# Gated mix of linear attention and SwiGLU: the last output tile in two column groups of 448 and 64 instead of three, its first group evicted by two engines

## The chip, the cores and the metric

The kernel runs on one core of a Trainium2 chip. A core has five engines that run side by side and meet at semaphores: TensorE (PE in the profile: matmuls; PEld: the weight loads that go ahead of them), VectorE (DVE), ScalarE (ACT), GpSimd (POOL) and SyncE (SP), which here only issues DMAs. ScalarE can issue DMAs as well; ACTq and SPq are the two queues from which they are issued here. Matmuls write to PSUM[...] from which VectorE or ScalarE must copy ("evict") a result to SBUF[...].

The metric is the device time of one execution in microseconds (us); lower is better.

## The reference

All inputs and the output are bf16. The input x has 2048 rows (tokens) of 512 columns.

```python
x = A_x
g = _sigmoid((x * gate_w).sum(-1, keepdims=True))
a = _A_ref(x, A_wqkv, A_wo)      # linear attention, 32 heads of 16
b = _B_ref(x, B_w1, B_w3, B_w2)  # (silu(x @ w1) * (x @ w3)) @ w2, F = 1376
return g * a + (1 - g) * b

# _A_ref: q, k, v = x @ wqkv, split into heads
phi = lambda t: jnp.where(t > 0, t + 1, jnp.exp(t)) + 1e-6
pq, pk = phi(q), phi(k)
kv = jnp.einsum("bhsd,bhse->bhde", pk, v)
z = jnp.einsum("bhsd->bhd", pk)
num = jnp.einsum("bhqd,bhde->bhqe", pq, kv)
den = jnp.einsum("bhqd,bhd->bhq", pq, z)[..., None] + 1e-6
o = num / den                    # back to (S, D), then o @ wo
```

## The kernel before

The 2048 rows are 16 tiles of 128 (NT), in four blocks of 512 (NTB blocks, TPB = 4 tiles each). A first stage computes k for all tiles, phi(k), and the sum of x^T phi(k) over the rows; from it and the weights wv and wo it folds attention into one 512x512 matrix W_sb. Then each block runs the feed-forward part (emit_ffn: gate and up matmuls at L312 and L320, tanh on ScalarE, two VectorE operations that leave hT) and, tile by tile, the output (emit_out). Between these stands the preparation of the next block (emit_q, emit_rem, emit_den, emit_norm). After the last block's feed-forward there is nothing left to prepare, so the program ends with four calls of emit_out, for tiles 12 to 15, one behind the other.

TensorE's instructions are issued in the order in which the program writes them (a manual schedule for PE); the other engines follow by semaphores that a tile framework places, from which instruction reads or writes which buffer. An engine takes its instructions in its own fixed order: one that waits holds up those behind it.

emit_out computes a tile's 128x512 output as 15 matmuls that add up in one PSUM tile o_ps: four with the attention features (pqT by W_sb, L353), one with the remainder of F (hTr by w2r_sb, L357), ten with hT by w2_sb (L362). The factor omg, one value per row, is applied in the eviction. For tiles 0 to 14 this is one column group of 512, evicted by ScalarE (L367, row o_out) and stored by SP (L378, 128 KB). For the last tile (t = 15) the columns are cut into three groups, 0 to 256, 256 to 448 and 448 to 512, each with its own 15 matmuls, its own PSUM tile, its eviction and its store:

```python
parts = [(0, h, True), (h, q7, True), (q7, D, True)]      # L344: h = 256, q7 = 448
o_ps = psX.tile([P, b - a], FP32, tag=f"XP{2 + (tt + i) % 2}", name="o_ps")   # L351
eng = nc.scalar if i == 1 else nc.sync                    # L377
```

The groups' PSUM tiles alternate between the buffers XP3, XP2 and XP3. The first two groups are evicted by ScalarE (L367), the third by VectorE (L371, a tensor_scalar with omg). The first and third are stored from SP's queue, the second from ScalarE's (L378). The SBUF tile is o_last. The program ends (L509) when SP has seen every store landed and the engines have met at closing semaphores.

Of the kernel before, what the change touches and what calls it, by code (L numbers as in the profile page):

```python
# [8 lines left out]
ACT = mybir.ActivationFunctionType  # L9
ALU = mybir.AluOpType  # L10
# [3 lines left out]
BF16 = mybir.dt.bfloat16  # L14
# [3 lines left out]
def kernel(  # L18
# [12 lines left out]
    nc = tc.nc  # L31
    P = nc.NUM_PARTITIONS

    Bb, S, D = A_x.shape
# [4 lines left out]
    NT = S // P  # L39
# [10 lines left out]
    out2d = out.flatten_outer_dims()  # L50

    consts = ctx.enter_context(tc.tile_pool(name="consts", bufs=1))
# [26 lines left out]
    TF = 2  # L79
    x_first = x2d[0 : TF * P, :].rearrange("(p j) d -> p j d", j=TF)  # L80
    out_first = out2d[0 : TF * P, :].rearrange("(p j) d -> j p d", j=TF)
# [6 lines left out]
        out=xT[:, :, TF * P : TB], in_=x2d[TF * P : TB, :], transpose=True  # L88
    )
    for tb in range(1, NTB):  # L90
        dq.dma_start(
            out=xT[:, :, tb * TB : (tb + 1) * TB], in_=x2d[tb * TB : (tb + 1) * TB, :],
# [7 lines left out]
    with nc.allow_non_contiguous_dma(reason="one gate weight per partition and chunk"):  # L100
        dq.dma_start(
            out=wr_sb[:, :, 2 * FR : NR], in_=gate_w.rearrange("(kc d o) -> d kc o", d=P, o=1)
        )
    dq.dma_start(out=wv_sb[:], in_=wqkv_r[:, :, 2 * D : 3 * D])
    for fsl in (slice(0, FM // 2), slice(FM // 2, FM)):
# [13 lines left out]
        out=bm, in_=bm, pattern=[[-Dh, HPC], [0, Dh]], compare_op=ALU.is_ge, fill=0.0,  # L119
# [3 lines left out]
        out=bm, in_=bm, pattern=[[Dh, HPC], [0, Dh]], compare_op=ALU.is_ge, fill=0.0,  # L123
# [6 lines left out]
    omg = consts.tile([P, NT], FP32, name="omg")  # L130
# [171 lines left out]
    def emit_ffn(tb, fc, between=None):  # L302
# [30 lines left out]
            out=st[tb, "hT"][:, fc, :], in0=up_ps[:], in1=gs[:], op=ALU.mult  # L333
        )

    def emit_out(tb, tt):
        t = tb * TPB + tt
        tsl = slice(tt * P, (tt + 1) * P)

        if t < NT - 1:  # L340
            parts = [(0, D, True)]
        else:
            h, q7 = D // 2, 7 * D // 8
            parts = [(0, h, True), (h, q7, True), (q7, D, True)]  # L344
        if t < NT - 1:
            o_out = work.tile([P, D], BF16, tag="o_out", name="o_out")
        else:
            o_out = consts.tile([P, D], BF16, name="o_last")
        lo = 0
        for i, (a, b, store) in enumerate(parts):  # L350
            o_ps = psX.tile([P, b - a], FP32, tag=f"XP{2 + (tt + i) % 2}", name="o_ps")  # L351
            for c in range(KC):
                nc.tensor.matmul(  # L353
                    o_ps[:], lhsT=st[tb, "pqT"][:, c, tsl], rhs=W_sb[:, c, a:b],
                    start=(c == 0), stop=False,
                )
            nc.tensor.matmul(  # L357
                o_ps[:], lhsT=st[tb, "hTr"][:, tsl], rhs=w2r_sb[:, a:b],
                start=False, stop=False,
            )  # L360
            for fc in range(FC):
                nc.tensor.matmul(  # L362
                    o_ps[:], lhsT=st[tb, "hT"][:, fc, tsl], rhs=w2_sb[:, fc, a:b],
                    start=False, stop=(fc == FC - 1),
                )
            if i < 2:
                nc.scalar.activation(  # L367
                    out=o_out[:, a:b], in_=o_ps[:], func=ACT.Copy, scale=omg[:, t : t + 1]
                )
            else:  # L370
                nc.vector.tensor_scalar(  # L371
                    out=o_out[:, a:b], in0=o_ps[:], scalar1=omg[:, t : t + 1], scalar2=None,
                    op0=ALU.mult,
                )
            if store:
                rows = out_first[t] if t < TF else out2d[t * P : (t + 1) * P, :]
                eng = nc.scalar if i == 1 else nc.sync  # L377
                eng.dma_start(out=rows[:, lo:b], in_=o_out[:, lo:b])  # L378
                lo = b


    k0 = [psM.tile([P, D], FP32, tag="mm", name=f"k0_{t}") for t in range(TPB)]
# [21 lines left out]
    with tc.manual_schedule(engines={ENG.DVE}):  # L404
# [18 lines left out]
        for dc in range(KC):  # L423
# [9 lines left out]
            out=z_sb[:].rearrange("p (b f) -> p b f", f=Q),  # L433
            in_=z_col[:, :, None].to_broadcast([P, NB, Q]),
        )
        kvT_ps = psX.tile([P, KC, P], FP32, tag="XP0", name="kvT_ps")
        for c in range(KC):
# [7 lines left out]
            out=kvT_sb[:], in0=kvT_ps[:],  # L445
# [22 lines left out]
    for tb in range(NTB):  # L468
        for fc in range(FC if tb == 0 else 0, FC):
            emit_ffn(tb, fc)  # L470
        nx = tb + 1
        for tt in range(TPB):
            if nx < NTB:
                emit_q(nx, tt, psX, "XP0")
                if tt % 2 == 0:
                    emit_rem(nx, tt // 2, psX, "XP1")
                    if tt == 2:
                        emit_omg(nx)
            emit_out(tb, tt)
            if nx < NTB:  # L480
                emit_den(nx, tt)
        if nx < NTB:
            emit_norm(nx)
# [30 lines left out]
```

## Time and profile before

| what | value |
|---|---|
| median of 5 runs | 179.13 us (178.62 to 179.45) |
| profiled execution, its own time | 179.45 us |
| its span, first to last instruction | 177.7 us |
| TensorE clock granted | 0.998 |
| PE busy | 174.3 us, 98% of the span, 883 matmuls |
| DVE, ACT, POOL busy | 118.7, 65.5, 63.7 us |
| eviction of a 128x512 o_out (ACT) | 0.688 us |
| last tile's evictions | 0.473 (256, ACT), 0.421 (192, ACT), 0.284 (64, DVE) |
| store of 128 KB from issue to landing | 1.9 us, 15 of them |

Busy time is what an engine's instructions took; the span is what the profiler saw from the first to the last instruction, and the execution's own time is 1.7 us longer. A row of the profile names the line, the engine, the operation and what it writes and reads (out<-in). Durations of matmuls in rows are those of one matmul through the pipeline; in the chain of waits each step is only what it adds before the next can start, so a 512-column matmul is 379 ns in its row and about 216 ns in the chain. A row marked SPq or ACTq is the issue of a DMA by that engine's queue, not the transfer.

### The profile page before, as it was taken

The numbers are of one execution on the slowest core, as the hardware profiler recorded it, in microseconds if no ns is written. First come the engines' busy times: TensorE is split into PE (matmuls) and PEld (weight loads), VectorE is DVE, ScalarE is ACT, GpSimd is POOL, SyncE is SP. The second block draws the span as 40 slices with busy tenths as digits, with TensorE's granted clock in tenths as the row PEclk, the third lists the DMA queues.
The fourth block names the chain that finished last, engine by engine and source line by source line (L and its number), as shares of the span: only waits on it lengthen the run. The fifth ranks groups of instructions, "written<-read, shape, count | busy, mean of one in ns | idle before, by whom it ended". The sixth has DMA issues, their size and how long they took to land.

```text
span 177.7 us, 2473 instructions
## 1 busy us (share of the span) xinstructions
PE 174.3 (98%) x883; PEld 84.2 (47%) x883; DVE 118.7 (67%) x204; ACT 65.5 (37%) x123; POOL 63.7 (36%) x80
## 2 busy tenths in 40 slices
PE   8999999999999999999999999999999999999994
PEld 4444444474444545444454544444545444444463
DVE  0398667899999837498786375978764669786000
ACT  3542423476532333342333333342443333331222
POOL 6087765689154323262003232620032328100000
PEclk9999999999999999999999999999999999999999
DMA  5999999911005011123000111230001012200002
GB/s 171 221 308 226 295 325 360 348 58 29 10 0 115 3 44 33 44 59 89 0 0 10 38 37 37 59 90 6 0 7 50 24 51 74 63 0 0 30 30 63
DMA packets 30380, 15.14 MB, mean 85 GB/s; under 512 B 20928, under 2 KB 30240, under 8 KB 30368
## 3 DMA queue, kind: packets, MB, share of 16 engines
q1 hardware_dynamic: 29952, 14.67, 30.1%
q10 hardware_dynamic: 416, 0.31, 0.5%
q8 instruction: 7, 0.11, 0.3%
q14 instruction: 5, 0.04, 0.1%
HBM read 8.42 MB, written 2.10 MB: 59 GB/s over the span
## 4 chain that ended last, share of the span: by engine, by line
PE 98%; DVE 0%; issue 0%
PE o_ps L362 19%; PE up_ps L320 19%; PE gate_ps L312 19%; PE o_ps L353 8%; PE q_ps L217 8%; PE XP L204 8%; PE k_ps L184 6%; PE r_ps L241 3%; PE k L184 2%; PE o_ps L357 2%; PE warm L161 2%; PE kvT_ps L440 1%; PE W_ps L458 0%; PE xTp L174 0%; DVE o_last L371 0%
## 5 line engine op out<-in xcount | busy, mean ns | idle before, releaser
L320 PE MATMUL up_ps<-xT,w_sb 128*128 128x512 bf16 x160 | 41.1, 379 | 0.0
L312 PE MATMUL gate_ps<-xT,w_sb 128*128 128x512 bf16 x160 | 41.1, 379 | 0.0
L225 POOL TENSOR_TENSOR qz<-pq,z_sb 128x512 f32<-128x512 bf16 x16 | 18.5, 1161 | 58.0 <-DVE pq L145 58.0
L325 ACT ACTIVATE th<-gate_ps 128x512 bf16<-128x512 f32 x40 | 23.9, 597 | 39.1 <-PE gate_ps L312 38.7
L362 PE MATMUL o_ps<-w_sb,hT 128*128 128x512 bf16 (+3 forms) x180 | 37.5, 355 | 0.0
L327 DVE SCALAR_TENSOR_TENSOR gs<-th,gate_ps 128x512 bf16<-128x512 bf16 x40 | 27.3, 682 | 5.4 <-ACT th L325 5.1
L332 DVE TENSOR_TENSOR hT<-up_ps,gs 128x512 bf16<-128x512 f32 x40 | 27.7, 691 | 3.8
L142 DVE TENSOR_SCALAR phi_m<-phi_e 128x512 bf16<-128x512 bf16 x32 | 13.6, 426 | 21.7 <-ACT phi_e L140 21.6
L362 PEld LDWEIGHTS <-hT 128*128 128x128 bf16 x180 | 16.9, 98 | 17.8
L320 PEld LDWEIGHTS <-w_sb 128*128 128x128 bf16 x160 | 15.7, 98 | 18.9
L312 PEld LDWEIGHTS <-w_sb 128*128 128x128 bf16 x160 | 15.6, 98 | 18.6
L292 POOL TENSOR_TENSOR pqn<-pq,rden 128x512 bf16<-128x512 bf16 x16 | 16.5, 1055 | 15.1 <-DVE rden L285 13.1
L367 ACT ACTIVATE o_out<-o_ps,omg 128x512 bf16<-128x512 f32 x15 | 10.3, 688 | 28.9 <-PE o_ps L362 28.9
L194 POOL TENSOR_TENSOR pks<-pks,pk_sb 128x512 f32<-128x512 f32 x15 | 17.4, 1161 | 7.4 <-DVE pk_sb L145 6.7
L353 PE MATMUL o_ps<-W_sb,pqT 128*128 128x512 bf16 (+3 forms) x72 | 16.8, 355 | 0.0
L217 PE MATMUL q_ps<-wq_sb,xT 128*128 128x512 bf16 x64 | 16.4, 379 | 0.0
L204 PE MATMUL XP<-pk_sb,x_sb 128*128 128x512 bf16 x64 | 16.3, 379 | 0.0
L228 DVE TENSOR_REDUCE den<-qz 128x32 f32<-128x512 f32 x16 | 10.9, 684 | 7.9 <-POOL qz L225 7.8
L140 ACT ACTIVATE phi_e<-k_ps 128x512 bf16<-128x512 f32 x12 | 7.2, 597 | 14.4 <-PE k_ps L184 14.4
L140 ACT ACTIVATE phi_e<-q_ps 128x512 bf16<-128x512 f32 x16 | 9.6, 597 | 7.8 <-PE q_ps L217 7.7
L184 PE MATMUL k_ps<-wk_sb,xT 128*128 128x512 bf16 x48 | 12.3, 379 | 0.0
L145 DVE SCALAR_TENSOR_TENSOR pq<-q_ps,phi_m 128x512 bf16<-128x512 f32 x16 | 11.1, 691 | 0.5
(60 smaller groups left out, 120.8 us busy)
## 6 DMA issues: line engine op xcount, KB each, us to landing
w_sb<-in_B_w_dram SPq DMA_DIRECT2D x4, 640.0 KB, 8.7
out_dram<-o_out SPq DMA_DIRECT2D x15, 128.0 KB, 1.9
w_sb<-in_B_w_dram SPq DMA_DIRECT2D x1, 1280.0 KB, 11.7
x_sb<-in_A_x_dram SPq DMA_DIRECT2D x2, 512.0 KB, 4.3
x_sb<-in_A_x_dram SPq DMA_DIRECT2D x1, 768.0 KB, 5.1
wq_sb<-in_A_wqkv_dram SPq DMA_DIRECT2D x1, 512.0 KB, 4.9
wv_sb<-in_A_wqkv_dram SPq DMA_DIRECT2D x1, 512.0 KB, 6.0
wo_sb<-in_A_wo_dram SPq DMA_DIRECT2D x1, 512.0 KB, 11.1
```

The costliest lines, as they stand in the source:

```text
L184: nc.tensor.matmul(k_ps[:], lhsT=xT[:, kc, t * P : (t + 1) * P], rhs=wk_sb[:, kc, :], start=(kc == 0), stop=(kc == KC - 1),)
L194: nc.gpsimd.tensor_add(pks[:], pks[:], pk_sb[:, t, :])
L204: nc.tensor.matmul(XP_ps[dc][:], lhsT=x_sb[:, t, dc * P : (dc + 1) * P], rhs=pk_sb[:, t, :], start=(t == 0), stop=(t == NT - 1),)
L217: nc.tensor.matmul(q_ps[:], lhsT=xT[:, kc, ts_tok], rhs=wq_sb[:, kc, :], start=(kc == 0), stop=(kc == KC - 1),)
L225: nc.gpsimd.tensor_tensor(out=qz[:], in0=st[tb, "pq"][:, tt, :], in1=z_sb[:], op=ALU.mult)
L312: nc.tensor.matmul(gate_ps[:], lhsT=w1_sb[:, kc, fsl], rhs=xT[:, kc, tok_sl], start=(kc == 0), stop=(kc == KC - 1),)
L320: nc.tensor.matmul(up_ps[:], lhsT=w3_sb[:, kc, fsl], rhs=xT[:, kc, tok_sl], start=(kc == 0), stop=(kc == KC - 1),)
L325: nc.scalar.activation(out=th[:], in_=gate_ps[:], func=ACT.Tanh, scale=0.5)
L327: nc.vector.scalar_tensor_tensor(out=gs[:], in0=th[:], scalar=1.0, in1=gate_ps[:], op0=ALU.add, op1=ALU.mult)
L332: nc.vector.tensor_tensor(out=st[tb, "hT"][:, fc, :], in0=up_ps[:], in1=gs[:], op=ALU.mult)
L353: nc.tensor.matmul(o_ps[:], lhsT=st[tb, "pqT"][:, c, tsl], rhs=W_sb[:, c, a:b], start=(c == 0), stop=False,)
L362: nc.tensor.matmul(o_ps[:], lhsT=st[tb, "hT"][:, fc, tsl], rhs=w2_sb[:, fc, a:b], start=False, stop=(fc == FC - 1),)
```

## The change

Only emit_out is changed, and of what it emits only the last tile. The columns are cut into two groups, 0 to 448 and 448 to 512, with 15 matmuls each (30 where there were 45). The first group's PSUM tile (XP3) is evicted in two pieces: columns 0 to 256 by ScalarE, then stored from ScalarE's queue, and columns 256 to 448 by VectorE, then stored from SP's queue. The second group, of 64 columns (now in XP2), is evicted by VectorE and stored by SP, as its counterpart before. For tiles 0 to 14 the same instructions are emitted as before.

```diff
-        if t < NT - 1:
-            parts = [(0, D, True)]
+        last = t == NT - 1
+        h, q7 = D // 2, 7 * D // 8
+        groups = [(0, q7), (q7, D)] if last else [(0, D)]
+        pieces = (
+            {0: [(0, h, nc.scalar, nc.scalar), (h, q7, nc.vector, nc.sync)],
+             q7: [(q7, D, nc.vector, nc.sync)]}
+            if last
+            else {0: [(0, D, nc.scalar, nc.sync)]}
+        )
+        if last:
+            o_out = consts.tile([P, D], BF16, name="o_last")
         else:
-            h, q7 = D // 2, 7 * D // 8
-            parts = [(0, h, True), (h, q7, True), (q7, D, True)]
...
-        for i, (a, b, store) in enumerate(parts):
+        for i, (a, b) in enumerate(groups):
             o_ps = psX.tile([P, b - a], FP32, tag=f"XP{2 + (tt + i) % 2}", name="o_ps")
...
-            if i < 2:
-                nc.scalar.activation(
-                    out=o_out[:, a:b], in_=o_ps[:], func=ACT.Copy, scale=omg[:, t : t + 1]
-                )
-            else:
-                nc.vector.tensor_scalar(
-                    out=o_out[:, a:b], in0=o_ps[:], scalar1=omg[:, t : t + 1], scalar2=None,
-                    op0=ALU.mult,
-                )
-            if store:
-                rows = out_first[t] if t < TF else out2d[t * P : (t + 1) * P, :]
-                eng = nc.scalar if i == 1 else nc.sync
-                eng.dma_start(out=rows[:, lo:b], in_=o_out[:, lo:b])
-                lo = b
+            for lo, hi, evac, queue in pieces[a]:
+                if evac is nc.scalar:
+                    nc.scalar.activation(
+                        out=o_out[:, lo:hi], in_=o_ps[:, lo - a : hi - a], func=ACT.Copy,
+                        scale=omg[:, t : t + 1],
+                    )
+                else:
+                    nc.vector.tensor_scalar(
+                        out=o_out[:, lo:hi], in0=o_ps[:, lo - a : hi - a],
+                        scalar1=omg[:, t : t + 1], scalar2=None, op0=ALU.mult,
+                    )
+                queue.dma_start(out=out2d_rows(t)[:, lo:hi], in_=o_out[:, lo:hi])
```

out2d_rows(t) gives a tile's rows of the output, as the two branches did before.

More of the change, by code (lines that the diff above doesn't have):

```diff
@@ L334, in emit_ffn, with out2d_rows @@
         )
+    def out2d_rows(t):
+        return out_first[t] if t < TF else out2d[t * P : (t + 1) * P, :]
     def emit_out(tb, tt):
@@ L338, in emit_out @@
         tsl = slice(tt * P, (tt + 1) * P)
-        if t < NT - 1:
-            parts = [(0, D, True)]
-        else:
-            h, q7 = D // 2, 7 * D // 8
-            parts = [(0, h, True), (h, q7, True), (q7, D, True)]
-        if t < NT - 1:
+        last = t == NT - 1
[9 more added lines that the diff above has]
+            o_out = consts.tile([P, D], BF16, name="o_last")
+        else:
             o_out = work.tile([P, D], BF16, tag="o_out", name="o_out")
-        else:
-            o_out = consts.tile([P, D], BF16, name="o_last")
-        lo = 0
-        for i, (a, b, store) in enumerate(parts):
+        for i, (a, b) in enumerate(groups):
             o_ps = psX.tile([P, b - a], FP32, tag=f"XP{2 + (tt + i) % 2}", name="o_ps")
@@ L365, in emit_out @@
                 )
-            if i < 2:
-                nc.scalar.activation(
-                    out=o_out[:, a:b], in_=o_ps[:], func=ACT.Copy, scale=omg[:, t : t + 1]
-                )
-            else:
-                nc.vector.tensor_scalar(
-                    out=o_out[:, a:b], in0=o_ps[:], scalar1=omg[:, t : t + 1], scalar2=None,
-                    op0=ALU.mult,
-                )
-            if store:
-                rows = out_first[t] if t < TF else out2d[t * P : (t + 1) * P, :]
-                eng = nc.scalar if i == 1 else nc.sync
-                eng.dma_start(out=rows[:, lo:b], in_=o_out[:, lo:b])
-                lo = b
+            for lo, hi, evac, queue in pieces[a]:
[10 more added lines that the diff above has]
+                queue.dma_start(out=out2d_rows(t)[:, lo:hi], in_=o_out[:, lo:hi])
     k0 = [psM.tile([P, D], FP32, tag="mm", name=f"k0_{t}") for t in range(TPB)]
```

## The prediction, made before the result was known

> **What bounds the kernel now.** I read the clock view first (0.998, so no throttling has to be allowed for), then the page's chain of waits: TensorE carries 98% of it, so only two things can change the time, the length of the TensorE stream and what comes behind its last matmul. The change touches the last output tile alone, so I read the last seven microseconds. The chain in order of time, whose columns are start in us, length in us and what ran:
>
> ```profile
> 170.96 0.86 PE o_ps L362 x4
> 171.82 0.44 PE o_ps L353 x4
> 172.26 0.11 PE o_ps L357
> 172.37 1.09 PE o_ps L362 x10
> 173.46 0.33 PE o_ps L353 x4
> 173.79 0.08 PE o_ps L357
> 173.88 0.82 PE o_ps L362 x10
> 174.70 0.12 PE o_ps L353 x4
> 174.82 0.03 PE o_ps L357
> 174.84 0.31 PE o_ps L362 x10
> 175.15 0.03 issue
> 175.18 0.28 DVE o_last L371
> ```
>
> The reader is to see three groups of 15 matmuls without a gap: 256 columns in 1.64 us (0.44+0.11+1.09), 192 in 1.23 us, 64 in 0.46 us. The last ends at 175.15. Behind it stand one short eviction by VectorE and a store. The evictions and store issues, from the timeline by engine (start, length):
>
> ```profile
> 173.50 0.47 ACT L367 ACTIVATE o_last<-o_ps,omg 128x256 bf16<-128x256 f32 x1 [0.95 <-PE o_ps L362]
> 174.74 0.42 ACT L367 ACTIVATE o_last<-o_ps,omg 128x192 bf16<-128x192 f32 x1 [0.76 <-PE o_ps L362]
> ...
> 174.00 0.33 SPq L378 DMA_DIRECT2D out_dram<-o_last  x1
> ...
> 175.19 0.36 ACTq L378 DMA_DIRECT2D out_dram<-o_last  x1
> 175.49 0.33 SPq L378 DMA_DIRECT2D out_dram<-o_last  x1
> ```
>
> Each group's eviction and store lie under the next group's matmuls; after 175.15 only the 64-column eviction (0.28) and its store are bare. The table of DMA issues (KB, us from issue to landing) and SP's own waits close the picture:
>
> ```profile
> out_dram<-o_last SPq DMA_DIRECT2D x1, 64.0 KB, 2.1
> out_dram<-o_last ACTq DMA_DIRECT2D x1, 48.0 KB, 1.6
> out_dram<-o_last SPq DMA_DIRECT2D x1, 16.0 KB, 1.4
> ...
> SPq L509 <- DMA out_dram<-o_last: 0.6, 1, 0.6
> ```
>
> The 48 KB store lands at 175.19+1.6 = 176.8, the 16 KB one at 175.49+1.4 = 176.9, and the program's end (L509) waits for both. From 176.9 to the span's end at 177.7 there is a fixed 0.8 us of closing semaphores that the change leaves alone. So the end is set by when SP issues its last store.
>
> **What the Trainium skill says.** "PSUM — Partial Sum Buffer", section "PSUM bank collisions raise a hardware error": two engines may not access one bank on the same partitions at once, reads against reads included, and software has to guard a bank with semaphores. The trace of before has no two engines reading one o_ps tile, so it can neither confirm nor deny this; but it decides whether the two pieces of the 448 group can be evicted side by side. "VectorE: DVE Perf Modes", section "Why PSUM operands drop a tier": an fp32 PSUM operand keeps VectorE at its basic rate, and its "Specifications" give 0.96 GHz, so 128 more columns cost an estimated 0.133 us. The trace agrees roughly: the row gsr (L251, 128x192) takes 0.345 us and pq (L145, 128x512) 0.691, or 0.139 us for 128 columns. "DMA: Bandwidth & Descriptors", section "Issuing engines are not separate DMA queues": a second issuing queue saves only issue time. Here that is 0.33 us a store.
>
> **The change part by part.**
>
> TensorE. The 256 and 192 groups become one of 448. From the rows, a 512-column matmul advances the chain by 0.216 us (0.86/4), a 256-column one by 0.109 (1.64/15); on the line between them 448 columns cost 0.189, and 15 of them 2.84 us, against 1.64+1.23 = 2.87. Gain 0.03 us. The 15 weight loads that go were hidden (the row PEld is always beside PE). The 448 group ends at 174.67, the 64 group at 175.12. The 64 group now takes the PSUM buffer XP2 instead of XP3; its earlier owner is the tile before, evicted from 171.86 to 172.55, long before 174.67, so this wait costs nothing, and PE doesn't stop.
>
> ScalarE. It starts the 256-column piece 0.04 us behind the group as before (173.46 to 173.50): at 174.71, ends at 174.71+0.47 = 175.18. Before, the same piece was done at 173.97, under matmuls. It loses the 192 piece (0.42).
>
> VectorE. In the changed program's instruction order the 192-column eviction does not wait for PE but for ScalarE, and the semaphore's value is the one that the 256 piece sets. So the pieces run one behind the other, as the PSUM page asks. A wait of VectorE on ScalarE costs 0.03 us (phi_e 21.24+0.60, phi_m at 21.87), so it starts at 175.21. Its length isn't in the trace: the 64-column row of the same operation takes 0.284, and 128 columns more cost 0.139 or 0.133: 0.42. Bounds: 0.345, the row of that width at L251, and 0.45. I take 0.42, so it ends at 175.63. Queued behind it on VectorE is the 64-column eviction, whose matmuls are ready at 175.12 and which ran at 175.18 before. Independent VectorE instructions overlap by 0.08 us in the timeline (gsr 38.57+0.34, next at 38.83), so it ends at 175.84, or at 175.94 if it follows with a 0.03 gap. SP waits for it.
>
> SP. The 256 store leaves SP's queue for ScalarE's: it issues at 175.21 instead of 174.00. With the longest landing that the table shows for 64 KB, 2.1, it lands at 177.3. The 192 store moves from ScalarE's queue to SP's: SP starts 0.03 us behind an eviction (175.46, 175.49), hence 175.66, and is busy with it until 175.99. Only then can the 64 store be issued. Between two SP issues, the second of which also waits for its own DMA semaphore, the timeline shows 0.09 us (a transpose from 131.43 for 2.40 ends at 133.83, the next store starts at 133.92). So 175.99+0.09 = 176.08. The 64 eviction, ready at 175.84 to 175.94, hides under this.
>
> Sum. The last store is issued at 176.08 instead of 175.49: +0.59 us. With 1.4 us to landing it lands at 177.5, behind the 256 store (177.3), so that one is covered by 0.2 us. The chain of additions to compare: -0.03 (TensorE), then the 256 eviction 0.47, wait 0.03, 192 eviction 0.42, SP issue 0.33 and gap 0.09, in place of the 64 group and its eviction. The span goes from 177.74 to 178.33 and the profiled execution from 179.45 to 180.04; the median of the five runs, 179.13, is 0.32 lower than that execution, and the same addition gives 179.72 us, +0.33%.
>
> Unknowns: the 192 eviction (-0.08 to +0.03); SP's second issue, which took 0.53 instead of 0.33 where a store followed close behind transposes (row 133.92 in the timeline), 0 to +0.2; landing of a 16 KB store right behind a 48 KB one on its own queue, not in the trace. Before, the 16 KB store had 48 KB of another queue ahead of it, 0.30 us earlier, so I take 1.4 again, with -0.3 to +0.3 around it.
>
> **The rivals.** What a measurement of this kernel can tell from no change is about 0.3%, 0.54 us; the forecast stands just outside.
>
> A, the same mechanism with dearer stores: the second issue takes 0.53 and the landing is 0.2 longer, as three stores now end together with 128 KB in flight instead of 64. 179.13+0.59+0.2+0.2 = 180.1. For it: landings of the 128 KB o_out stores reach 3.3 us. Against: the DMA share at the end is low, 0.31 from 176 to 177 us.
>
> B, not slower: the end is carried by completion. The 192 store goes through SP's queue 0.42 us ahead of the 64 one and leaves the DMA rings running, so the last store lands sooner after its issue. If 1.4 becomes 0.8, the move of 0.59 is paid back: 179.13+0.59-0.60 = 179.1. It decides from a landing under 0.81 us. Against it: no store of o_out or o_last landed under 1.4.
>
> C, the wait doesn't bind: the two pieces are evicted side by side. Then VectorE's 192 piece runs from 174.71 to 175.13, the SP issues stand at 175.16 and 175.58 (+0.09), and the 256 store, 175.21+2.1 = 177.3, is the later by 0.4 in the worst case: 179.2 to 179.5. Against it: the wait is in the program.
>
> **How the numbers follow.** The serial chain at its own price, +0.4 to +0.75: 0.74, of which 0.52 comes out above 0.54 us as measured and 0.22 within it, since the medians themselves move by about 0.2 (runs from 178.62 to 179.45). A: 0.12, all slower. B: 0.07, of which 0.02 faster by over 0.3%, 0.05 within. C: 0.07, within. Slower 0.64, same 0.34, faster 0.02. Forecast 179.72. The range leaves out B's lower part and A's upper one: 179.3 to 180.15.
>
> **What would show each step right or wrong.** The 448 matmuls advancing by 0.189 us and the stream ending 0.03 earlier; the 192 eviction starting 0.03 behind the 256 one's end and not beside it; its length near 0.42; the SP stores 0.42 apart, the second at about 176.1; the 64 eviction finished before SP is free; landing of the last store near 1.4, and the tail of 0.8 unchanged. The prediction is wrong if VectorE starts at 174.7, if the stores land in under 1 us, or if the 256 store on ScalarE's queue lands last.

## The result, and the profile after

| | before | with the change |
|---|---|---|
| median | 178.97 us (80 runs, 178.49 to 179.85) | 179.66 us (43 runs, 179.11 to 181.3) |
| ratio to before | | 1.0041, 95% interval 1.0031 to 1.0050 |
| profiled execution, span | 179.45, 177.7 us | 179.79, 178.1 us |

The change makes the kernel slower by 0.4%, some 0.7 us. A ratio of 1 lies outside the interval. The five runs that the prediction started from had a median of 179.13; 80 runs give 178.97.

The chain of waits of the changed kernel, in order of time (start in us, length, what):

```profile
172.47 1.91 PE o_ps L368 x10
174.38 0.03 issue
174.40 0.48 ACT o_last L374
174.88 0.03 issue
174.91 0.42 DVE o_last L379
175.33 0.19 DVEq L513
```

Before, the chain ran through TensorE to the last matmul and left it for one eviction of 0.28 us. Now it leaves TensorE one column group earlier, at 174.38, goes through ScalarE's 256 columns, and then, behind them, through VectorE's 192. The last group's matmuls are no longer on it. (DVEq L513 is the end of VectorE's program, which comes when the 64-column eviction is done.) The timeline by engine:

```profile
174.20 0.28 PE L359 MATMUL o_ps<-W_sb,pqT 128*128 128x64 bf16 x4
...
174.40 0.47 ACT L374 ACTIVATE o_last<-o_ps,omg 128x256 bf16<-128x256 f32 x1 [2.15 <-PE o_ps L368]
174.91 0.42 DVE L379 TENSOR_SCALAR o_last<-o_ps,omg 128x192 bf16<-128x192 f32 x1 [11.81 <-ACT o_last L374]
...
174.91 0.36 ACTq L383 DMA_DIRECT2D out_dram<-o_last  x1
...
175.35 0.33 SPq L383 DMA_DIRECT2D out_dram<-o_last  x1
...
175.78 0.38 SPq L383 DMA_DIRECT2D out_dram<-o_last  x1
```

The bracket on the DVE row is the line to look for: VectorE had been idle for 11.81 us and was released by ScalarE's o_last, not by PE. SP's two stores stand 0.43 us apart.

The span depends on the whole program, its start too: in this execution the last tile began 0.30 us earlier than in the profile of before. To compare ends I therefore count from an event just ahead of the change, SP's issue of the store of tile 14, which is line one of before and line two of after:

```profile
172.58 0.33 SPq L378 DMA_DIRECT2D out_dram<-o_out  x1
```

```profile
172.28 0.33 SPq L383 DMA_DIRECT2D out_dram<-o_out  x1
```

Counted from there (the common clock of what follows), with the trace's nanoseconds, the last store is issued at 2.91 us before and 3.50 after (+0.59), it lands 1.44 and 1.48 us later (+0.04; landings on this clock are counted to the end of SP's closing wait for them, 0.02 us behind the landing itself), and the span ends at 5.16 and 5.81 (+0.65). So 0.59 of the 0.65 is already there when the last store is issued. TensorE itself is 0.035 us earlier (its last matmul starts at 2.331 instead of 2.366).

One profile is one execution, but the span of every execution is on record, to 0.1 us: 109 of before and 44 of the change. The mean span grows from 177.29 to 177.88, by 0.59 us (95% interval 0.45 to 0.73, by resampling the executions). The mean time grows by 0.72, so 0.13 of it lies outside the span. That part of an execution was 1.76 us on average before and never over 1.9; with the change it is 1.89 on average, and over 1.9 in 16 of the 44 executions. No trace covers it and its cause stays open. It is seen in e2, e3, e4, e5 and e7 below, whose last tile has 30 matmuls as in the change, and not in e1 and e6, which have 45 as before.

### The profile page after: what moved, and what is told of

Read it like the earlier page. It is cut to its first block, busy times and chain, and to the rows that moved or that the text cites. A ratio compares the mean times of both kernels' runs of the same rounds, so it can differ in the third digit from the quotient of the medians.

```text
span 178.1 us, 2442 instructions
## 1 busy us (share of the span) xinstructions
PE 173.8 (98%) x868; PEld 82.3 (46%) x868; DVE 120.3 (68%) x205; ACT 65.0 (36%) x122; POOL 63.6 (36%) x80
## 4 chain that ended last, share of the span: by engine, by line
PE 94%; DMA 3%; SPq 0%; ACT 0%; DVE 0%; issue 0%; DVEq 0%
PE gate_ps L312 19%; PE up_ps L320 19%; PE o_ps L368 19%; PE XP L204 8%; PE q_ps L217 8%; PE o_ps L359 8%; PE k_ps L184 6%; PE r_ps L241 3%; DMA xT<-in_A_x_dram 3%; PE o_ps L363 2%; PE k L184 1%; PE kvT_ps L444 1%; PE W_ps L462 0%; ACT o_last L374 0%; DVE o_last L379 0%; SPq L84 0%
## 5 line engine op out<-in xcount | busy, mean ns | idle before, releaser
L368 PE MATMUL o_ps<-w_sb,hT 128*128 128x512 bf16 (+2 forms) x170 | 37.3, 367 | 0.0
L142 DVE TENSOR_SCALAR phi_m<-phi_e 128x512 bf16<-128x512 bf16 x32 | 15.2, 475 | 20.1 <-ACT phi_e L140 20.1
L368 PEld LDWEIGHTS <-hT 128*128 128x128 bf16 x170 | 16.0, 98 | 18.6
L359 PE MATMUL o_ps<-W_sb,pqT 128*128 128x512 bf16 (+2 forms) x68 | 16.6, 366 | 0.0
```

The source lines that it names most:

```text
L359: nc.tensor.matmul(o_ps[:], lhsT=st[tb, "pqT"][:, c, tsl], rhs=W_sb[:, c, a:b], start=(c == 0), stop=False,)
L368: nc.tensor.matmul(o_ps[:], lhsT=st[tb, "hT"][:, fc, tsl], rhs=w2_sb[:, fc, a:b], start=False, stop=(fc == FC - 1),)
```

## The experiments

Three things changed together: two engines share a PSUM tile, two of the three stores go through SP, and three stores end together. (A fourth, fewer column groups, is rival U in e4.) Theory W says that the wait on the shared tile carries the loss. Rival S says that the bunched stores do. All kernels are the changed one with the edit shown, and all ratios are to runs of before on the same chip. Times on the common clock come from one profiled execution of each kernel; where the mean span of all executions says more, it is given beside them.

**e1_two_banks**: the first stretch of 448 columns in 30 matmuls instead of 15, alternating between two PSUM buffers, so that each evicting engine has its own.

```diff
-            o_ps = psX.tile([P, b - a], FP32, tag=f"XP{2 + (tt + i) % 2}", name="o_ps")
+            cuts = [(a, h), (h, b)] if last and i == 0 else [(a, b)]
+            tags = [f"XP{2 + (tt + i) % 2}", "XP0"]
+            banks = [
+                (lo, hi, psX.tile([P, hi - lo], FP32, tag=tag, name="o_ps"))
+                for (lo, hi), tag in zip(cuts, tags)
+            ]
...
+                for lo, hi, o_ps in banks:
+                    nc.tensor.matmul(
+                        o_ps[:], lhsT=st[tb, "pqT"][:, c, tsl], rhs=W_sb[:, c, lo:hi],
```

> The 448 columns stay one stretch of 30 matmuls, but the 256 and the 192 columns lie in two PSUM buffers (XP3 and XP0) and their matmuls alternate; evicting engines and store queues are those of the change. VectorE then has no reason to wait for ScalarE. Theory W (the wait on the shared PSUM tile carries the loss): the 192 eviction starts beside the 256 one and ends 0.45 us earlier than in the change, the 64 one follows when its matmuls are done, and SP, still busy with the 192 store, issues the last store about 0.12 us later than before: +0.1 to +0.25 us over before, 0.4 to 0.5 under the change. Rival S (three stores bunched at the end, two of them on SP's queue, are what costs, whatever the evictions do): +0.6 as with the change. Rival T (the wait comes from the shared SBUF tile o_last): the wait stays, +0.6.

Measured: 179.24 us, ratio 1.0015 (1.0002 to 1.0029), against 1.0041 (1.0031 to 1.0050) for the change. Its timeline:

```profile
174.56 0.47 ACT L383 ACTIVATE o_last<-o_ps,omg 128x256 bf16<-128x256 f32 x1 [2.11 <-PE o_ps L376]
175.07 0.38 ACTq L392 DMA_DIRECT2D out_dram<-o_last  x1
...
174.65 0.42 DVE L388 TENSOR_SCALAR o_last<-o_ps,omg 128x192 bf16<-128x192 f32 x1 [11.34 <-PE o_ps L376]
...
175.09 0.33 SPq L392 DMA_DIRECT2D out_dram<-o_last  x1
```

Here VectorE is released by PE, and its eviction runs beside ScalarE's with the same lengths as when they stood in line (0.42 and 0.47). Two engines writing different columns of o_last don't wait for each other, so rival T falls. On the common clock the last store is issued at 3.03: 0.47 earlier than in the change, 0.12 later than before, as W had it. The loss shrinks to 0.15%, with the three stores still bunched and two of them on SP's queue; that speaks against S as the whole cause. By mean spans it shrinks from 0.59 to 0.27 us, so a good half of it goes with the wait; the 45 matmuls also take back TensorE's 0.035 (the last starts at 2.368). Not as expected is the landing of the last store, 1.63 us instead of 1.44, which puts the profiled end 0.31 us behind that of before, over the 0.25 that W allowed; the last pair of experiments takes it up.

**e2_queues**: the change with before's queues.

```diff
-            {0: [(0, h, nc.scalar, nc.scalar), (h, q7, nc.vector, nc.sync)],
+            {0: [(0, h, nc.scalar, nc.sync), (h, q7, nc.vector, nc.scalar)],
```

> The change with the store queues of before: 256 from SP, 192 from ScalarE's queue, 64 from SP; the evictions as in the change. Theory W: the evictions still stand one behind the other and the 64 one ends at the same time as in the change, but SP is free by then, so its last store is issued some 0.23 us earlier than in the change: +0.35 to +0.45 us over before. Rival S: with one SP store bare at the end as before, most of the loss goes: 0 to +0.1 us.

Measured: 179.73 us, ratio 1.0040 (1.0021 to 1.0060). From its timeline:

```profile
175.39 0.42 DVE L379 TENSOR_SCALAR o_last<-o_ps,omg 128x192 bf16<-128x192 f32 x1 [11.81 <-ACT o_last L374]
...
176.02 0.33 SPq L383 DMA_DIRECT2D out_dram<-o_last  x1
```

The trace shows what was foreseen at the issue: VectorE waits as in the change, the 64 eviction ends where it did, SP is free, and the last store goes out at 3.27 on the common clock, 0.23 earlier than in the change and 0.36 later than before. It lands in 1.56 us instead of 1.48, so the profiled end is 5.65, 0.16 earlier than in the change. In the times this gain doesn't show. In the mean spans it does (0.41 us over before instead of 0.59), but with intervals that overlap (0.19 to 0.66 and 0.45 to 0.73), so how much the queues are worth rests on the trace: 0.23 us at the issue, 0.16 at the end. The profiled end is 0.49 over before, a little more than W's 0.45. That most of the loss stays with SP's second store out of the way contradicts S, which expected 0 to 0.1.

**e3_one_piece**: the 448 columns evicted by ScalarE alone.

```diff
-            {0: [(0, h, nc.scalar, nc.scalar), (h, q7, nc.vector, nc.sync)],
+            {0: [(0, q7, nc.scalar, nc.scalar)],
```

> The 448 columns evicted in one piece by ScalarE and stored in one piece (112 KB) from ScalarE's queue; the 64 group as in the change. Eviction estimated at 0.63 us (0.473 for 256 columns, 0.688 for 512), so it ends 0.29 us before the 192 piece of the change did, and VectorE's 64 eviction waits for matmuls alone. Theory W: the 112 KB store, issued about 0.12 us before the last store of before but with 1.7 to 1.9 us to landing, ends the program: +0.15 to +0.35 us over before. Rival S (two stores in place of three, one on each queue): no loss, 0 to +0.1.

Measured: 179.78 us, ratio 1.0047 (1.0030 to 1.0063); as slow as the change. Both theories were too low. The rows of its timeline:

```profile
174.38 0.64 ACT L374 ACTIVATE o_last<-o_ps,omg 128x448 bf16<-128x448 f32 x1 [2.15 <-PE o_ps L368]
175.04 0.38 ACTq L383 DMA_DIRECT2D out_dram<-o_last  x1
175.12 0.33 SPq L383 DMA_DIRECT2D out_dram<-o_last  x1
```

and of its table of DMA issues (KB, us from issue to landing):

```profile
out_dram<-o_last ACTq DMA_DIRECT2D x1, 112.0 KB, 1.8
out_dram<-o_last SPq DMA_DIRECT2D x1, 16.0 KB, 1.9
```

The eviction was sized rightly (0.63 expected). SP's small store was issued at 2.87 on the common clock, even earlier than before's 2.91, but it took 1.91 us to land beside the 112 KB of the other queue and landed last, at 4.78. I had taken it to land in 1.4 and to be covered. So leaving out the wait is not enough. That the large store beside it delayed the small one is not tested here by taking it away; e6 does that for e1.

**e5_dve_first**: the two pieces in the other order.

```diff
-            {0: [(0, h, nc.scalar, nc.scalar), (h, q7, nc.vector, nc.sync)],
+            {0: [(h, q7, nc.vector, nc.sync), (0, h, nc.scalar, nc.scalar)],
```

> The change with the order of the two pieces turned round: VectorE's 192 piece first, then ScalarE's 256 piece, which then waits for VectorE; queues as in the change. Theory W: the 64 eviction is no longer behind the wait; SP issues the last store about 0.08 us later than before, and the program's end passes to the 256 store, issued about 175.66 on the clock of before's profile with 1.6 to landing: +0.25 to +0.4 us over before. Rival S: three stores bunched as in the change, +0.6. If the 64 store on SP ends the program all the same: +0.1.

Measured: 179.49 us, ratio 1.0034 (1.0017 to 1.0052).

```profile
174.37 0.47 ACT L374 ACTIVATE o_last<-o_ps,omg 128x256 bf16<-128x256 f32 x1 [2.60 <-DVE o_last L379]
174.87 0.37 ACTq L383 DMA_DIRECT2D out_dram<-o_last  x1
...
174.36 0.33 SPq L383 DMA_DIRECT2D out_dram<-o_last  x1
```

The wait has turned round: now ScalarE is released by VectorE's o_last. SP's last store is issued at 2.99 on the common clock, 0.08 later than before as worked out, and the program's end has passed to ScalarE's 64 KB store, issued at 3.08 with 1.6 to landing. The profiled end, 5.58, is 0.42 over before, as is the mean span; the time's interval (0.3 to 0.9 us) holds that, but S's 0.6 too, so it is the trace that decides. Whichever engine goes first, the other's piece starts about half a us late (2.63 instead of 2.13 for VectorE in the change, 2.58 instead of 2.12 for ScalarE here).

**e4_384_128**: two groups whose first is evicted and stored under the second.

```diff
-        h, q7 = D // 2, 7 * D // 8
+        h, q7 = D // 2, 3 * D // 4
...
-            {0: [(0, h, nc.scalar, nc.scalar), (h, q7, nc.vector, nc.sync)],
+            {0: [(0, q7, nc.scalar, nc.sync)],
```

> Two column groups as in the change, but cut at 384: the first is evicted whole by ScalarE and stored by SP under the second group's matmuls, the second (128 columns) is evicted by VectorE and stored by SP. No PSUM tile is read by two engines and only one store is bare at the end. Theory W: as before within 0.1 us (the 30 matmuls gain 0.03 to 0.05, the wider last eviction costs 0.07). Rival U (fewer groups are themselves the loss, because more is left to evict and store behind a longer group): +0.4 us or more.

Measured: 179.43 us, ratio 1.0020 (1.0001 to 1.0038). The chain of waits of this kernel:

```profile
174.53 0.57 PE o_ps L368 x10
175.11 0.02 issue
175.13 0.35 DVE o_last L379
```

The shape of before is back: the chain stays on TensorE to its last matmul, and behind it stands one eviction. The last store is issued at 2.94 and the span ends at 5.28, both close to before (2.91 and 5.16); 0.06 of the 0.12 is one closing semaphore wait more behind the landing. The times can't tell W from U here: their interval, 0.02 to 0.68 us, holds both W's 0.1 and U's 0.4. Half of the mean excess lies outside the span; the mean span is 0.22 over before (-0.01 to 0.48). So it is the trace that speaks for W: what U expected to be left behind the last matmul isn't there. Two groups are no gain either: 0.03 us of matmuls is traded for 0.07 of a wider last eviction.

**e6_two_banks_less_store and e7_change_less_store** take the 256-column store away and nothing else, e6 from e1 and e7 from the change:

```diff
+                if last and lo == 0:
+                    continue
                 queue.dma_start(out=out2d_rows(t)[:, lo:hi], in_=o_out[:, lo:hi])
```

> The kernel with two PSUM buffers (e1_two_banks) without the store of columns 0 to 256 of the last tile, which stay unwritten; their eviction is kept. There the last store needed 1.63 us to land, against 1.44 before. If the other queue's 64 KB, in flight at the same time, is what held it up, the landing falls back to 1.40 to 1.50 and the end behind the last tile but one comes 0.15 us earlier than in e1_two_banks. If SP's own 48 KB store just ahead of it does it, 1.6 stays.

> The change without the store of columns 0 to 256 of the last tile, which stay unwritten; their eviction is kept, and with it VectorE's wait. Theory W: this store is covered in the change (it lands before the last one), so the loss stays: +0.55 to +0.65 us over before. Rival S (bunched transfers): with 64 KB fewer in flight at the end the loss falls to +0.3 or less.

Measured: e6 179.13 us, ratio 1.0009 (0.9995 to 1.0024); e7 179.64 us, ratio 1.0039 (1.0024 to 1.0053). The stores of e1 and then of e6 (KB, us from issue to landing):

```profile
out_dram<-o_last ACTq DMA_DIRECT2D x1, 64.0 KB, 1.9
out_dram<-o_last SPq DMA_DIRECT2D x1, 48.0 KB, 1.7
out_dram<-o_last SPq DMA_DIRECT2D x1, 16.0 KB, 1.6
```

```profile
out_dram<-o_last SPq DMA_DIRECT2D x1, 48.0 KB, 1.5
out_dram<-o_last SPq DMA_DIRECT2D x1, 16.0 KB, 1.5
```

In e6 the last store, issued at the same place as in e1 (3.03), lands in 1.48 us instead of 1.63: the other queue's 64 KB was what held it up, not SP's own 48 KB ahead of it. This rests on one profiled execution of each kernel; the times don't tell e6 from e1. Its end comes only 0.08 earlier than in e1 and not 0.15, because with one store fewer a closing wait of 0.06 falls behind the landing. In e7 the last store is issued at 3.50 and lands in 1.48 us, both as in the change, and the loss stays (mean span 0.56 over before; the profiled end, 0.71 over before, again holds the closing wait of 0.06). With 64 KB fewer in flight nothing is won: this refutes S for the transfers of the change, where that store is covered. What is left of S is SP's own second store, and e2 puts it at 0.23 us of the last issue.

Put together, on the common clock:

| kernel | last SP issue | its landing | end of span | mean span over before's | ratio (95%) |
|---|---|---|---|---|---|
| before | 2.91 | 1.44 | 5.16 | | |
| the change | 3.50 | 1.48 | 5.81 | 0.59 | 1.0041 (1.0031 to 1.0050) |
| e1, own PSUM buffers | 3.03 | 1.63 | 5.47 | 0.27 | 1.0015 (1.0002 to 1.0029) |
| e2, queues of before | 3.27 | 1.56 | 5.65 | 0.41 | 1.0040 (1.0021 to 1.0060) |
| e3, one piece | 2.87 | 1.91 | 5.66 | 0.74 | 1.0047 (1.0030 to 1.0063) |
| e5, VectorE first | 2.99 | (ScalarE's store ends it) | 5.58 | 0.42 | 1.0034 (1.0017 to 1.0052) |
| e4, 384 and 128 | 2.94 | 1.46 | 5.28 | 0.22 | 1.0020 (1.0001 to 1.0038) |
| e6, e1 less a store | 3.03 | 1.48 | 5.40 | 0.23 | 1.0009 (0.9995 to 1.0024) |
| e7, change less a store | 3.50 | 1.48 | 5.88 | 0.56 | 1.0039 (1.0024 to 1.0053) |

Of the 0.59 us by which the last issue is late, 0.47 goes with the wait (e1); the other 0.12 is SP's 192 store, which then still stands in the way (0.23 while the wait is there, by e2). No variant was faster than the kernel before: fewer matmuls save TensorE's 0.035 us, and each way to them here cost more.

## Why the prediction was right

The measured ratio, +0.41% or some 0.7 us, lies in the range that the prediction gave to the serial chain (+0.4 to +0.75), for the reason given. That the two medians almost agree (179.72 forecast, 179.66 measured) is in part luck: the base of five runs was 0.16 us above that of 80 runs, the addition 0.10 below the difference of the medians, and the two errors nearly cancel. By the prediction's steps:

- TensorE: 0.189 us a 448-column matmul was forecast; the trace steps by 0.189, and the stream ends 0.035 earlier (0.03 forecast). PE did not stop before the 64 group.
- The wait: forecast 0.03 us behind ScalarE's end, measured 0.03 (174.40+0.47 to 174.91). With the wait taken away by separate PSUM buffers, the last issue comes 0.47 earlier and 0.32 of the 0.59 us of mean span returns.
- The 192-column eviction, which was in no trace: 0.42 forecast, 0.418 measured.
- The 64-column eviction starts 0.08 before the 192 one ends, as the gsr rows suggested, and is done 0.26 us before SP takes its store. It was hidden, and SP's issue of the 192 store was what it hid under; with that store moved away (e2) the last issue moves up by 0.23.
- SP's two stores: 0.42 apart forecast, 0.425 measured. The second took 0.38 to issue, where rival A had feared 0.53.
- The sum to the last issue: +0.59 forecast, +0.592 measured. The mean span, over all executions, grew by the same 0.59.

Three terms were mis-sized, all small. The landing behind it was taken as unchanged and came 0.04 longer, and some 0.01 to 0.02 more went into the closing waits: 0.65 in the trace instead of 0.59. The time outside the span, which the same addition took as unchanged, grew by 0.13 on average, for a reason that is open. And the 256 store was taken to need up to 2.1 us to land, its figure from before, which left a cover of 0.2 us; it took 1.6 and landed 0.8 before the last one. The figure of 2.1 belonged to another place, on SP's queue behind the 128 KB of tile 14; whether that is what made it long is not shown.

Rival A (dearer stores) is not what happened in the change, though its mechanism is real in e1, where the landing of 1.63 falls to 1.48 with the other queue's store taken away (e6); the 1.91 of e3 fits it. Rival B needed a landing under 0.81; none was under 1.4. Rival C is what e1 built, and its worst case, the 256 store ending the program, didn't come about.

## What to carry to other kernels

Splitting an eviction over two engines gained nothing here while both pieces lay in one PSUM tile: the program made the second engine wait for the first, whichever was first, and the two pieces in line took longer than one (0.47 and 0.42 us against 0.64 for all 448 columns, e3). The wait was in the program; what would happen without it on one tile no run shows. Give each engine its own PSUM buffer (e1, whose mean span is still 0.27 us over that of before), or stagger the column groups so that each eviction and store lies under the next group's matmuls, which is what the three groups did. At the end of a program look at three things in order: the last eviction, whether the issuing engine is still busy with another store when it is ready, and what else is in flight when that store goes out.

## What the runs showed of the hardware that was not expected

How long the last 16 KB store took to land went with what else was in flight. It took 1.44 to 1.48 us in before, the change, e6 and e7, with 48 KB issued 0.30 to 0.43 us ahead of it, on the other queue or on its own. It took 1.56 us in e2, with 48 KB on the other queue 0.19 us ahead, and 1.52 us in e5, with 64 KB on the other queue issued 0.09 us behind it besides the 48 KB on its own. In e1 it took 1.63 us, with 64 KB on the other queue 0.45 us ahead besides the 48 KB on its own, and in e3 1.91 us, with 112 KB on the other queue 0.09 us ahead. Removing the 64 KB alone brought 1.63 back to 1.48. Only this last step was tested by taking something away, and each figure is one execution.
